# A shared ring for dwq and wq, four dK store buffers, and V^T of five batches by TensorE instead of by a transposing load

## The chip, the cores and the metric

One core of one Trainium2 chip. The metric is the device time of one execution in microseconds; a kernel's time is the median of several executions. Executions are compared with the kernel before on the same chip, in the same rounds. The chips differ: the kernel before takes 1650 us on some and 1642 on others, so ratios carry further here than times.

## The reference, cut to what matters

Two independent attention blocks A and B, whose outputs are concatenated, with all gradients. For each block, 8 batches of 96 queries, 32 heads of 128, 512 cached keys, model width 640, all bf16:

```python
q = (x @ wq).reshape(B, Sq, H, Dh).transpose(0, 2, 1, 3)
p = softmax(einsum("bhqd,bhkd->bhqk", q, k_cache) * Dh ** -0.5)
o = einsum("bhqk,bhkd->bhqd", p, v_cache)
out = o.transpose(0, 2, 1, 3).reshape(B, Sq, H * Dh) @ wo
# returned: out of both blocks, and the gradients of x, k_cache, v_cache, wq, wo of each
```

## The kernel before: the parts that the change touches

Heads go in pairs; a batch of a pair takes two ticks, some 6 us. Every transfer goes through one SyncE queue in program order. K and V come twice: natural, and transposed by the load. A transposing load of a pair, as this kernel makes it and reads it with correct results, leaves the keys in a peculiar order: 64 groups of 16, eight of one head and eight of the other.

```python
def p_ldT(h, b, which):          # KT or VT of two heads by a transposing load
    t_ = kvp.tile([128, F4 * KC, 16], BF16, name=key + "_p", bufs=5 if which == 0 else 4)
    sp(nc.sync.dma_start_transpose(t_[:], src))
    half = t_[:, :, j * R8:(j + 1) * R8]      # for each of the two heads: 8 of every 16
    CS[...][key] = half.rearrange("p (f c) r -> p f c r", c=KC)

def c_s6(h, b):                  # dP = dO V^T ; dS = (dP - dl) * P, reading dP in steps
    nc.tensor.matmul(dP_ps[:], hs["dOT_h"][:, tok], st["VT"], start=True, stop=True)
    nc.vector.scalar_tensor_tensor(dS_sb[:].rearrange("q (a f) -> q a f", f=F4),
        dP_ps[:].rearrange("q (f a) -> q a f", f=F4), dl_ps[:, 0:1], P_sb..., ...)

def c_s7(h, b):                  # dK of a pair, evacuated by ACT, stored by SyncE
    st["dK_p"] = wk.tile([128, HP, KC * 128], BF16, name="dK_sb", bufs=3)
def qD(h, c_lo, c_hi):           # dwq of a pair
    pr["dwq_sb"] = hd.tile([128, DC, HP * 128], BF16, name="dwq_sb", bufs=1)
# ... (the rest of the attention, projections and weight gradients left out)
```

## Time and profile before

| | before |
|---|---|
| median of 3 executions | 1650.46 us (1649.55 to 1652.88) |
| profiled execution, span | 1640.3 us |
| TensorE busy | 98% |
| granted clock, mean | 0.996 |

The lines that show the bound, the stretches and the stops stand in the prediction below. The columns are: line, engine, operation, output<-input, shapes, count | busy us, mean ns of one | idle us of the engine just before them, and what ended most of it.

```profile
L458 ACT ACTIVATE dK_sb<-dK_ps 128x512 bf16<-128x512 f32 x512 | 305.4, 597 | 149.6 <-PE dK_ps L453 130.9 <-DMA out_dram<-dK_sb 10.6 <-PE optp_ps L362 2.2
L362 PE MATMUL optp_ps<-PT_sb,V_sb 128*128 128x96 bf16 x2048 | 169.6, 204 | 3.0 <-ACT PT_sb L376 0.9 <-DMA V_sb<-in_A_v_cache_dram 0.8 <-DMA V_sb<-in_B_v_cache_dram 0.5
```

ACT waited 10.6 us in all for stores of dK, which is what the fourth buffer is for. TensorE waited almost nowhere for V loads: 3.0 us ahead of 512 products O^T.

### The profile page before, as it was taken

What the parts mean: (1) busy time and instruction counts of PE and PEld (TensorE: products, weight loads), DVE (VectorE), ACT (ScalarE), POOL (GpSimd) and SP (SyncE); (2) the same over time, 40 slices, a digit from 0 to 9 for tenths busy, and PEclk for the clock granted to TensorE, in tenths of its full rate; (3) what the DMA queues carried; (4) which work ended last, traced back from release to release, by engine and by line L of the source; (5) the groups of instructions that cost most, each with busy time, mean ns of one, the idle gap of its engine ahead of it and who ended that gap; (6) DMA issues with size and microseconds to landing.
All of it is one profiled execution on the core that took longest, in us unless ns stands there. A gap on an engine that the chain in (4) does not pass through costs nothing.

```text
span 1640.3 us, 55387 instructions
## 1 busy us (share of the span) xinstructions
PE 1602.0 (98%) x20713; PEld 1262.0 (77%) x20906; DVE 1340.0 (82%) x3406; ACT 1346.9 (82%) x3498; POOL 532.3 (32%) x1026
## 2 busy tenths in 40 slices
PE   8899999999999999999999999999999999999998
PEld 6777877878777787777777778777787777877776
DVE  5876888888888888878778778888888888888796
ACT  7889988879788788877868889788788888889783
POOL 1333333333333333333323333333333333333331
PEclk9999999999999999999999999999999999999999
DMA  9999999999999999999999999999999999999995
GB/s 263 261 293 273 292 291 282 275 275 279 276 292 289 290 280 282 280 276 258 284 289 311 289 288 273 290 290 283 275 287 278 272 290 287 281 292 285 284 267 167
DMA packets 375566, 458.12 MB, mean 279 GB/s; under 512 B 40704, under 2 KB 367104, under 8 KB 367104
## 3 DMA queue, kind: packets, MB, share of 16 engines
q1 hardware_dynamic: 375296, 454.57, 103.2%
q8 instruction: 163, 2.67, 0.7%
q14 instruction: 107, 0.88, 0.1%
HBM read 160.10 MB, written 159.12 MB: 195 GB/s over the span
## 4 chain that ended last, share of the span: by engine, by line
PE 89%; DMA 4%; ACT 4%; issue 2%; DVE 1%; SPq 0%; POOL 0%; ACTq 0%; DVEq 0%
PE o_ps L536 12%; PE q_ps L250 12%; PE dwq_ps L511 6%; PE dK_ps L453 6%; PE dV_ps L387 6%; PE S_ps L314 6%; PE dwo_ps L491 6%; PE dP_ps L411 6%; PE optp_ps L362 5%; PE optp_ps L369 5%; PE dq_dst_ps L430 5%; PE dq_dst_ps L437 5%; PE n_ps L265 3%; PE nat_ps L477 2%; DMA out_dram<-dK_sb 2%
## 5 line engine op out<-in xcount | busy, mean ns | idle before, releaser
L401 POOL TENSOR_TENSOR prod<-OT_h,dOT_h 128x96 bf16<-128x96 bf16 x512 | 187.1, 365 | 824.4 <-DVE rinv L336 438.2
L346 POOL TENSOR_SCALAR P_sb<-E_sb,rinv 96x512 bf16<-96x512 bf16 x508 | 349.8, 689 | 252.5 <-DVE rinv L336 252.1
L458 ACT ACTIVATE dK_sb<-dK_ps 128x512 bf16<-128x512 f32 x512 | 305.4, 597 | 149.6 <-PE dK_ps L453 130.9
L326 ACT ACTIVATE E_sb<-S_ps,negm 96x512 bf16<-96x512 f32 x512 | 350.9, 685 | 65.1 <-DVE negm L316 51.8
L316 DVE TENSOR_REDUCE negm<-S_ps 96x1 f32<-96x512 f32 x512 | 347.6, 679 | 67.2 <-PE S_ps L314 66.5
L415 DVE SCALAR_TENSOR_TENSOR dS_sb<-dP_ps,dl_ps,P_sb 96x512 bf16<-96x512 f32 x512 | 380.6, 743 | 1.6 <-PE optp_ps L369 1.4
L392 ACT ACTIVATE dV_sb<-dV_ps 128x512 bf16<-128x512 f32 x512 | 307.2, 600 | 3.9 <-PE dV_ps L387 2.6
L376 ACT ACTIVATE PT_sb<-optp_ps 128x384 bf16<-128x384 bf16 x512 | 255.2, 499 | 1.7 <-PE optp_ps L369 0.8
L439 DVE COPY dST_sb<-dq_dst_ps 128x384 bf16<-128x384 bf16 x512 | 177.5, 347 | 53.1 <-PE dq_dst_ps L437 51.5
L387 PE MATMUL dV_ps<-dOnat_h,P_sb 96*128 96x128 bf16 x2048 | 199.7, 219 | 2.1 <-DVE ob L546 1.0
L453 PE MATMUL dK_ps<-Qnat_h,dS_sb 96*128 96x128 bf16 x2048 | 198.9, 219 | 0.1
L411 PE MATMUL dP_ps<-VT_p,dOT_h 128*96 128x512 bf16 x512 | 195.8, 382 | 0.0
L314 PE MATMUL S_ps<-KT_p,QT_h 128*96 128x512 bf16 x512 | 194.0, 379 | 0.5 <-ACT E_sb L326 0.2
L453 PEld LDWEIGHTS <-dS_sb 96*128 96x128 bf16 x2048 | 147.5, 97 | 48.3 <-issue 0.6
L430 PE MATMUL dq_dst_ps<-dST_sb,K_sb 128*128 128x96 bf16 x2048 | 171.8, 205 | 3.0 <-ACT dK_sb L458 2.8
L369 PE MATMUL optp_ps<-ident,P_sb 96*128 96x96 bf16 x2048 | 172.4, 206 | 2.2 <-DVE P_sb L346 1.6
L362 PE MATMUL optp_ps<-PT_sb,V_sb 128*128 128x96 bf16 x2048 | 169.6, 204 | 3.0 <-ACT PT_sb L376 0.9
L437 PE MATMUL dq_dst_ps<-ident,dS_sb 96*128 96x96 bf16 x2048 | 171.8, 205 | 0.0
L536 PE MATMUL o_ps<-wo_r,OT_h 128*128 128x128 bf16 (+1 forms) x722 | 144.5, 294 | 2.4
L536 PE MATMUL o_ps<-wqT_h,dQT_h 128*128 128x512 bf16 (+1 forms) x720 | 144.2, 294 | 2.5
L362 PEld LDWEIGHTS <-V_sb 128*128 128x128 bf16 x2048 | 107.6, 96 | 50.7 <-issue 3.4
L491 PE MATMUL dwo_ps<-g_nat,Onat 128*128 128x128 bf16 (+1 forms) x735 | 129.4, 297 | 4.3 <-ACT dK_sb L458 2.6
(75 smaller groups left out, 3044.7 us busy)
## 6 DMA issues: line engine op xcount, KB each, us to landing
out_dram<-dV_sb SPq DMA_DIRECT2D x256, 256.0 KB, 4.4
out_dram<-dK_sb SPq DMA_DIRECT2D x256, 256.0 KB, 4.5
V_sb<-in_A_v_cache_dram SPq DMA_DIRECT2D x128, 256.0 KB, 4.3
K_sb<-in_A_k_cache_dram SPq DMA_DIRECT2D x128, 256.0 KB, 4.4
V_sb<-in_B_v_cache_dram SPq DMA_DIRECT2D x128, 256.0 KB, 4.3
K_sb<-in_B_k_cache_dram SPq DMA_DIRECT2D x128, 256.0 KB, 4.3
out_dram<-ob SPq DMA_DIRECT2D x88, 160.0 KB, 4.1
out_dram<-dwq_sb SPq DMA_DIRECT2D x32, 320.0 KB, 4.9
```

The source lines that it names most:

```text
L314: nc.tensor.matmul(S_ps[:], hs["QT_h"][:, tok], st["KT"], start=True, stop=True)
L316: nc.vector.tensor_reduce(negm[:], S_ps[:], axis=AX.X, op=ALU.max, negate=True)
L326: nc.scalar.activation(E_sb[:].rearrange("q (a f) -> q a f", f=F4), st["S_ps"][:].rearrange("q (f a) -> q a f", f=F4), ACT.Exp, bias=st["n ...
L346: eng.tensor_scalar(P_sb[:], st["E_sb"][:], st["rinv"][:], 0.0, op0=ALU.mult, op1=ALU.add)
L362: nc.tensor.matmul(OT_ps, st["V_sb"][:, c, :], st["PT_sb"][:, c * Sq:(c + 1) * Sq], start=(c == 0), stop=(c == KC - 1))
L387: nc.tensor.matmul(dV_ps[:, c * 128:(c + 1) * 128], P_sb[:, c * 128:(c + 1) * 128], hs["dOnat_h"][:, b * 128:(b + 1) * 128], start=True, s ...
L392: nc.scalar.activation(dV_p[:, j], dV_ps[:], ACT.Identity, scale=1.0)
L411: nc.tensor.matmul(dP_ps[:], hs["dOT_h"][:, tok], st["VT"], start=True, stop=True)
L415: nc.vector.scalar_tensor_tensor(dS_sb[:].rearrange("q (a f) -> q a f", f=F4), dP_ps[:].rearrange("q (f a) -> q a f", f=F4), dl_ps[:, 0:1] ...
L453: nc.tensor.matmul(dK_ps[:, c * 128:(c + 1) * 128], dS_sb[:, c * 128:(c + 1) * 128], hs["Qnat_h"][:, b * 128:(b + 1) * 128], start=True, s ...
L458: nc.scalar.activation(dK_p[:, j], dK_ps[:], ACT.Identity, scale=1.0)
L536: nc.tensor.matmul(o_ps[:], src[:, t * 128:(t + 1) * 128], rhs, start=(hh == 0), stop=(hh == groups[g] - 1))
```

## The change

The intent is to take load off the SyncE queue in the passage from block 1 to block 2, and to let its lag show less. dwq shares the ring of wq tiles, which pays for a fourth dK buffer. V^T of five batches of the last pair of block 1 is made by TensorE from the natural V, which is loaded anyway. dwo rows of the last three pairs of block 1 are stored one tick sooner.

```diff
+    def p_vT(h, b):
+            t_ = kvp.tile([128, F4 * KC, 16], BF16, name="VT_p", bufs=4)
+            v_ps = bank([128, HP * KC * 128], BF16, "vT_ps")
+            ... 8 x nc.tensor.transpose(v_ps[...128 columns...], V_sb[:, c, :], ident[:])
+            for j in range(HP):
+                half = t_[:, :, j * R8:(j + 1) * R8].rearrange("p (f c) r -> p f c r", c=KC)
+                evac("act" if j == 0 else "dve", half.rearrange("p f c r -> p c r f"),
+                     v_ps[:, j * KC * 128:(j + 1) * KC * 128].rearrange("p (c r f) -> p c r f", c=KC, f=F4))
-  name="dK_sb", bufs=3            ->  +  name="dK_sb", bufs=4
-  name="dwq_sb", bufs=1           ->  +  name="wq_p", bufs=2
-  em.add(ct + OFF["vt"], SLOTS["LOAD"], p_ldT(h, b, 1))
+  p_vT at ct + 4 where (blk, h, b) in pools["vpe"], else as before
-  qB_st(h) at max(hk["qB"]) + 2   ->  +  + 1 for the last three pairs of block 1
+  pools["vpe"] = {(0, NH - HP, b) for b in range(5)}
```

(Shortened; the arrows stand for one removed and one added line.) The evacuation walks its output in the order c, r, f, so that consecutive elements, 2 bytes each, are KC x 16 = 64 elements, that is 128 bytes, apart.

More of the change, by code (lines that the diff above doesn't have):

```diff
@@ L291, in p_ldn, with f @@
         return f
+    def p_vT(h, b):
+        def f():
+            t_ = kvp.tile([128, F4 * KC, 16], BF16, name="VT_p", bufs=4)
+            v_ps = bank([128, HP * KC * 128], BF16, "vT_ps")
+            for j in range(HP):
+                V_sb = CS[(blk, h + j, b)]["V_sb"]
+                for c in range(KC):
+                    nc.tensor.transpose(v_ps[:, (j * KC + c) * 128:(j * KC + c + 1) * 128], V_sb[:, c, :], ident[:])
+            for j in range(HP):
+                half = t_[:, :, j * R8:(j + 1) * R8].rearrange("p (f c) r -> p f c r", c=KC)
+                CS[(blk, h + j, b)]["VT"] = half
+                evac("act" if j == 0 else "dve", half.rearrange("p f c r -> p c r f"), v_ps[:, j * KC * 128:(j + 1) * KC * 128].rearrange("p (c r f) -> p c r f", c=KC, f=F4))
+        return f
     def p_st(h, b, which):
@@ L455, in f @@
             if j == 0:
-                st["dK_p"] = wk.tile([128, HP, KC * 128], BF16, name="dK_sb", bufs=3)
+                st["dK_p"] = wk.tile([128, HP, KC * 128], BF16, name="dK_sb", bufs=4)
             dK_p = CS[(blk, h - j, b)]["dK_p"]
@@ L504, in f @@
             if "dwq_sb" not in pr:
-                pr["dwq_sb"] = hd.tile([128, DC, HP * 128], BF16, name="dwq_sb", bufs=1)
+                pr["dwq_sb"] = hd.tile([128, DC, HP * 128], BF16, name="wq_p", bufs=2)
             n = c_hi - c_lo
@@ L580, in build_block @@
                     em.add(tick0 - 13 if early and b == 0 else ct + (max(OFF["kt"], -1) if early else OFF["kt"]), SLOTS["LOAD"], p_ldT(h, b, 0))
-                    em.add(ct + OFF["vt"], SLOTS["LOAD"], p_ldT(h, b, 1))
+                    if (blk, h, b) in pools["vpe"]:
+                        em.add(ct + 4, SL_HEAD, p_vT(h, b))
+                    else:
+                        em.add(ct + OFF["vt"], SLOTS["LOAD"], p_ldT(h, b, 1))
                     em.add(ct + OFF["vn"], SLOTS["LOAD"] + 0.1, p_ldn(h, b, 1))
@@ L601, in build_block @@
                 em.add(c0t + hk["qB"][min(di, len(hk["qB"]) - 1)], SL_HEAD + 1, qB(h, di))
-            em.add(c0t + max(hk["qB"]) + 2, SL_LOAD + 0.3, qB_st(h))
+            em.add(c0t + max(hk["qB"]) + (1 if first and h >= H - 3 * HP else 2), SL_LOAD + 0.3, qB_st(h))
             em.add(c0t + hk["qA1"], SL_HEAD, qA(h, 1))
```

## The prediction

> **What bounds the kernel now.** I read the engine shares of the page first, then the chain that ended last, then a table of 41 us stretches, then the TensorE instructions in order of time, and last the DMA issues of SyncE in the same stretches.
>
> The page:
>
> ```profile
> span 1640.3 us, 55387 instructions
> ...
> PE 1602.0 (98%) x20713; PEld 1262.0 (77%) x20906; DVE 1340.0 (82%) x3406; ACT 1346.9 (82%) x3498; POOL 532.3 (32%) x1026
> ...
> PE 89%; DMA 4%; ACT 4%; issue 2%; DVE 1%; SPq 0%; POOL 0%; ACTq 0%; DVEq 0%
> ```
>
> TensorE is the bound: 98% busy, 89% of the chain. Only 38.3 us of the span (1640.3 - 1602.0) is without it, so no removed wait can give more than that, 2.3%, plus what a lowered clock costs. Where the 38 us lie, by stretches (columns: length, busy time of PE, its weight loads, DVE, ACT, POOL with counts, granted clock, DMA share, GB/s):
>
> ```profile
> 41.00:82.00 41.00, 36.49 (x497) 29.70 (x497) 33.16 (x85) 36.20 (x99) 15.54 (x30) 0.96 1.07 261
> 697.00:738.00 41.00, 40.68 (x502) 31.36 (x506) 32.08 (x83) 32.80 (x85) 12.62 (x25) 1.00 1.06 277
> 738.00:779.00 41.00, 37.63 (x518) 30.40 (x520) 35.73 (x90) 29.62 (x77) 12.92 (x25) 1.00 1.06 258
> 779.00:820.00 41.00, 38.23 (x491) 30.73 (x497) 29.96 (x75) 35.15 (x92) 13.21 (x25) 0.96 1.03 283
> 861.00:902.00 41.00, 38.43 (x523) 30.29 (x526) 35.27 (x92) 35.03 (x92) 14.60 (x28) 1.00 1.07 307
> 902.00:943.00 41.00, 38.94 (x484) 30.21 (x485) 29.87 (x74) 33.51 (x89) 12.49 (x24) 0.96 1.06 293
> ```
>
> An ordinary stretch (697 to 738) loses 0.3 us. The loss is in the first 123 us, in the passage from block 1 to block 2 (738 to 943), and in the drain. The DMA share is above 1 in all, so the transfer stream runs close to its own limit. The stops of TensorE in the passage (start, length, what, idle before, releaser):
>
> ```profile
> 779.23 1.84 PE L159 MATMUL tp_ps<-ident,ob 128*128 128x128 bf16 x15 [2.90 <-ACT ob L170]
> 793.92 0.44 PE L220 MATMUL woT_ps<-ident,wo_r 128*128 128x128 bf16 x5 [1.79 <-ACT dK_sb L458]
> 844.41 0.38 PE L387 MATMUL dV_ps<-dOnat_h,P_sb 96*128 96x128 bf16 x4 [0.98 <-DVE ob L546]
> 896.50 0.34 PE L362 MATMUL optp_ps<-PT_sb,V_sb 128*128 128x96 bf16 x4 [0.48 <-DMA V_sb<-in_B_v_cache_dram]
> 918.41 0.38 PE L491 MATMUL dwo_ps<-g_nat,Onat 128*128 128x512 bf16 x1 [1.69 <-ACT dK_sb L458]
> ```
>
> TensorE waits for an evacuation, which itself waits for a buffer to be stored. ACT shows it:
>
> ```profile
> 778.90 0.28 ACT L170 ACTIVATE ob<-dwo_ps 128x128 bf16<-128x128 f32 x1 [3.67 <-DMA out_dram<-ob]
> 793.27 0.60 ACT L458 ACTIVATE dK_sb<-dK_ps 128x512 bf16<-128x512 f32 x1 [1.97 <-DMA out_dram<-dK_sb]
> ```
>
> Why were the stores late? All transfers go through one SyncE queue in program order, and there:
>
> ```profile
> 770.47 1.54 SPq L277 DMA_TRANSPOSE VT_p<-in_A_v_cache_dram  x1
> 772.10 0.53 SPq L288 DMA_DIRECT2D K_sb<-in_A_k_cache_dram  x1
> 772.72 0.42 SPq L297 DMA_DIRECT2D out_dram<-dK_sb  x1
> 773.20 0.46 SPq L497 DMA_DIRECT2D out_dram<-ob  x1
> 773.75 1.42 SPq L141 DMA_DIRECT2D ob<-in_grad_out_dram  x3
> ```
>
> No gaps: the queue issues back to back, 1.1 us or more for a transposing load against 0.4 to 0.5 for a plain one. The dK pair finished by ACT at 773.6 is stored only at 787.70, 14 us later, while in calm stretches this lag is 2 to 8 us. So the queue is behind, by the extra loads of block 2, and three store buffers no longer cover the lag.
>
> [...] a dK store takes a median 4.5 us from issue to landing, and its buffer is held that long. [...] after 2.90 us idle, 15 transposes take 1.84 us, against 1.00 at 759.66; the 8 us from 775 and the 8 us from 919 (after only 1.69 us idle) have a granted clock of 0.79, which is 1.7 us lost in each. [...] eight transposes (n_ps) occupy the chain for 0.45 us, 56 ns each. [...]
>
> **The change, part by part.** I compared the order of instructions on each engine. POOL is unchanged; TensorE gains only the transposes; ACT and DVE each gain five copies and a few neighbours change places; SyncE loses five transposing loads, and stores of dwo rows of the last three pairs of block 1 move ahead of about three transfers.
>
> 1. dwq in the wq ring. It frees 128x5x256 bf16, 2560 bytes a partition, and pays for the fourth dK buffer, 2048 bytes. By the emission ticks a wq tile's last reader is three ticks (about 9 us) before its buffer is asked for again, and dwq still follows the previous dwq's store by eleven ticks. I expect no wait: 0 us.
>
> 2. Four dK buffers. Each gives two more ticks, about 6 us, between a store and the reuse. Stops put down to dK: 1.79 at 794, then 0.24 + 0.72 + 0.54 + 1.69 = 3.2 between 882 and 918 with 1.7 us of low clock behind the last. In the first 110 us 0.32 + 2.81 + 0.28 + 0.90, of which I count 1.2: the long one (2.81 at 71.97) is followed at once by a V load that lands just when it is used, so there the wait only changes its name.
>
> 3. V^T by TensorE. Added: 5 batches x 8 transposes x 56 ns = 2.24 us on the bound engine, in full. Added on ACT 5 x about 0.6 us (as dK's 128x512 copy, 597 ns), on DVE 5 x about 0.5 us (128x640 copies take 480, the scattered store may cost more): 3 us each over 34 us, on engines about 82% busy. I allow 0.5 us of TensorE for it, since ACT is full from 783 to 791. Removed: the five loads at 752.66, 761.79, 770.47, 778.01, 784.86, with issue times 1.10, 1.17, 1.54, 2.26, 2.12, 8.2 us of the queue, and about 5 us of DMA time (estimate: 256 KB at the mean 279 GB/s, 0.94 us each). So the gradient loads and stores from 773 on come 3 to 4 us sooner, later ones 5 to 8.
>
> 4. The dwo store one tick sooner: 773.20 becomes about 769, so its buffer is free when ACT asks at 775.2. With the gradient loads also sooner, the stop of 2.90 us and 1.7 us of low clock should go, and the 0.98 us at 844 (also a store of this ring).
>
> Gross gain: 2.9 + 1.7 (776) + 1.8 (794) + 1.0 (844) + 3.2 + 1.7 (882 to 918) + 1.2 (start) = 13.5 us. Taken back: 2.24 for transposes, 0.5 for evacuations, about 1 because the fourth batch's transposes follow the gradient transposes at once and their V load (issued 776.36, landing 781.7) would come 1 us late even when issued 3.5 us sooner, and about 1.5 from 882 to 914, where V loads land 0.05 to 0.9 us before use, so without the dK stops TensorE reaches those loads sooner. Net 13.5 - 5.2 = 8.3 us; I round to 9, because the sooner queue should cover part of that last item. 1650.5 - 9 = 1641.5 us.
>
> **Rivals.**
> - *The feed is the true bound of the passage.* If SyncE and DMA run flat out from 738 to 943, then freed buffers only let TensorE reach late loads. For it: no gaps in the queue, DMA share above 1, slack of V loads 0.05 us at 896.5. Against: at 846 to 860 V loads land 5 to 11 us ahead, so the feed catches up there, and the removed loads relieve the same feed. Then only the 776 and 844 parts remain against 2.2 of cost: about 1647.
> - *The transposes cost more than they free.* They need V_sb about half a tick sooner than the first reader did, take a PSUM bank out of eight, and load ACT at its fullest. Each batch could stop TensorE for 0.5 to 1 us: 3 to 5 us back, time 1644 to 1650.
> - *The shared ring waits.* If a wq load waited for a dwq store, each pair could lose a few tenths, about 30 times: 1645 to 1655. The ticks speak against it.
> - *Everything clears,* with the start's 2.81 and its low clock too: about 1635.
>
> **Range and chances.** 1635 (all clears) to 1648.5 (feed-bound or dear transposes) should hold 8 of 10. Faster by over 2% means below 1617, more than nearly all idle time, 1%; slower by over 2% needs a wait repeated in all 32 pairs, 1%; within 2%, 98%.
>
> **What would show it.** Right if the stops at 776, 794 and 918 are gone, no ACT wait for a dK store is left in the passage, and the stretches 779 to 820 and 902 to 943 have clock 1.00; the vT_ps matmuls should sum to about 2.2 us of chain. Step 2 is wrong if as much idle stands there with V_sb or K_sb loads as releaser; step 3 if vT transposes wait for V_sb or their copies delay PT_sb; step 1 if a dwq copy or wq load shows waits for the other. An unchanged or longer time would mean the feed, not the buffers, sets the passage.

## The result, and the profile after

| | before | after |
|---|---|---|
| median, same rounds, 6 executions each | 1651.56 us | 1664.96 us (1658.18 to 1671.43) |
| ratio of fast runs, 95% interval | | 1.0078 (1.0050 to 1.0106) |

A ratio is the mean time of one kernel's fast runs over that of the other's fast runs of the same rounds, so it is not quite the ratio of the medians. The change is within 2%, as predicted, but slower, not faster, and outside the range. All executions compared here were fast; the mean granted clock of the profiled one was 0.994.

The page of the profiled execution after:

```profile
span 1663.1 us, 55473 instructions
...
PE 1607.5 (97%) x20752; PEld 1266.1 (76%) x20946; DVE 1352.5 (81%) x3411; ACT 1362.2 (82%) x3503; POOL 533.3 (32%) x1026
...
PE 86%; DMA 6%; ACT 3%; DVE 2%; issue 2%; POOL 0%; SPq 0%; DVEq 0%; ACTq 0%
```

Beside the page before, TensorE is busy 5.5 us more (slower clock included), and its share of the chain fell from 89% to 86%. The same stretches as in the prediction:

```profile
738.00:779.00 41.00, 37.53 (x463) 28.67 (x468) 31.32 (x77) 32.12 (x72) 11.54 (x22) 1.00 1.05 279
779.00:820.00 41.00, 31.35 (x347) 24.52 (x348) 30.01 (x57) 29.50 (x60) 8.36 (x16) 0.83 0.74 195
902.00:943.00 41.00, 38.84 (x535) 31.20 (x538) 33.72 (x86) 37.02 (x100) 15.02 (x29) 1.00 1.10 298
```

The stretch 779 to 820, which by the prediction should have gone to a clock of 1.00, fell to 0.83 and 31.35 us busy, and the DMA share fell from 1.03 to 0.74: the feed now waits too. The stretch 902 to 943 did get its full clock. The groups that answer to those of before, and the new copies:

```profile
L472 ACT ACTIVATE dK_sb<-dK_ps 128x512 bf16<-128x512 f32 x512 | 305.8, 597 | 136.1 <-PE dK_ps L467 133.2
L376 PE MATMUL optp_ps<-PT_sb,V_sb 128*128 128x96 bf16 x2048 | 169.9, 204 | 20.9 <-DMA V_sb<-in_A_v_cache_dram 9.7 <-DMA V_sb<-in_B_v_cache_dram 5.0 <-DVE VT_p L173 2.0
L170 ACT ACTIVATE VT_p<-vT_ps 128x512 bf16<-128x512 bf16 x5 | 12.3, 2462 | 0.0
L173 DVE COPY VT_p<-vT_ps 128x512 bf16<-128x512 bf16 x5 | 12.2, 2437 | 8.5 <-ACT VT_p L170 8.5
```

ACT's 10.6 us of waits for dK stores are no longer listed: that mechanism works. But each V^T copy takes 2.46 us on ACT and 2.44 on DVE where 0.6 and 0.5 were put, DVE waits for ACT's, and TensorE is idle 20.9 us ahead of O^T, mostly for V loads. So the trace shows two suspects: the copies, and a feed of loads that is late all over the run. Also in it: DMA packets of 16 KB (the transposing loads) took 1297 ns in the mean, 1255 in the trace before.

### The profile page after: what moved, and what is told of

Read it like the earlier page. It is cut to its first block, busy times and chain, and to the rows that moved or that the text cites.

```text
span 1663.1 us, 55473 instructions
## 1 busy us (share of the span) xinstructions
PE 1607.5 (97%) x20752; PEld 1266.1 (76%) x20946; DVE 1352.5 (81%) x3411; ACT 1362.2 (82%) x3503; POOL 533.3 (32%) x1026
## 4 chain that ended last, share of the span: by engine, by line
PE 86%; DMA 6%; ACT 3%; DVE 2%; issue 2%; POOL 0%; SPq 0%; DVEq 0%; ACTq 0%
PE o_ps L550 12%; PE q_ps L250 11%; PE dV_ps L401 6%; PE dwq_ps L525 6%; PE dK_ps L467 6%; PE S_ps L328 6%; PE dP_ps L425 6%; PE dwo_ps L505 6%; PE optp_ps L376 5%; PE optp_ps L383 5%; PE dq_dst_ps L444 5%; PE dq_dst_ps L451 4%; PE n_ps L265 3%; PE nat_ps L491 3%; DMA V_sb<-in_A_v_cache_dram 2%; DMA V_sb<-in_B_v_cache_dram 2%
## 5 line engine op out<-in xcount | busy, mean ns | idle before, releaser
L376 PE MATMUL optp_ps<-PT_sb,V_sb 128*128 128x96 bf16 x2048 | 169.9, 204 | 20.9 <-DMA V_sb<-in_A_v_cache_dram 9.7
L550 PE MATMUL o_ps<-wqT_h,dQT_h 128*128 128x128 bf16 (+1 forms) x719 | 144.7, 295 | 2.5
L387 DVE CAST OT_h<-optp_ps 128x96 bf16<-128x96 f32 x512 | 125.1, 244 | 14.2 <-PE optp_ps L383 13.8
```

The costliest lines, as they stand in the source:

```text
L376: nc.tensor.matmul(OT_ps, st["V_sb"][:, c, :], st["PT_sb"][:, c * Sq:(c + 1) * Sq], start=(c == 0), stop=(c == KC - 1))
L550: nc.tensor.matmul(o_ps[:], src[:, t * 128:(t + 1) * 128], rhs, start=(hh == 0), stop=(hh == groups[g] - 1))
```

## The experiments

Sixteen runs were made, all with correct results. The table has fifteen of them; the before time is that of the same rounds.

| label | what | median us | before us | ratio, 95% interval |
|---|---|---|---|---|
| ring_only | shared ring alone | 1641.16 | 1641.24 | 0.9994 (0.9978 to 1.0010) |
| qb_only | sooner dwo store alone | 1640.16 | 1643.38 | 0.9989 (0.9975 to 1.0004) |
| no_vt | all but V^T by TensorE | 1639.12 | 1641.24 | 0.9985 (0.9973 to 0.9998) |
| vt_only | V^T by TensorE alone | 1655.44 | 1641.24 | 1.0079 (1.0059 to 1.0100) |
| after_again | the whole change | 1653.22 | 1641.89 | 1.0062 (1.0041 to 1.0083) |
| vt_dense | whole change, dense V^T | 1633.82 | 1641.24 | 0.9949 (0.9930 to 0.9968) |
| vt_swap | whole change, copy loops turned | 1633.17 | 1641.89 | 0.9943 (0.9924 to 0.9963) |
| vt_dense_only | dense V^T alone | 1635.53 | 1641.89 | 0.9965 (0.9949 to 0.9981) |
| vt_long | dense, copies repeated | 1644.41 | 1643.38 | 1.0011 (0.9995 to 1.0028) |
| vt_chunk | scattered, in four pieces | 1658.62 | 1650.30 | 1.0058 (1.0038 to 1.0078) |
| vt_later | scattered, DVE's copy later | 1648.73 | 1642.38 | 1.0043 (1.0028 to 1.0057) |
| vt_act | scattered, both on ACT | 1654.76 | 1642.38 | 1.0082 (1.0059 to 1.0105) |
| more_start | vt_swap, 9 batches | 1631.63 | 1643.38 | 0.9925 (0.9896 to 0.9954) |
| more_both | vt_swap, 13 batches | 1628.31 | 1643.38 | 0.9909 (0.9881 to 0.9937) |
| dense_both | vt_dense, 13 batches | 1635.39 | 1650.30 | 0.9909 (0.9894 to 0.9923) |

(before_again, a single execution for its trace, state unknown, took 1649.79 us.) The expectations of no_vt, vt_only, vt_dense and ring_only, in us, were written against the 1650 us of the first executions; on the chip of these runs the kernel before takes 1641, so ratios are to be compared. A first theory, A, says that the copies are the whole loss; B, that a slower feed from the ring or the fourth buffer is half of it; C, that the slower feed belongs to the execution and not to the program.

### Which part costs

**no_vt** and **vt_only** split the change in two.

```diff
  no_vt:    pools["vpe"] = set()                       # on the kernel after
  vt_only:  before + p_vT and pools["vpe"] of the kernel after; dK_sb bufs=3, dwq_sb bufs=1
```

> The changed kernel without the five V^T by TensorE (shared ring, four dK buffers and the earlier dwo store stay). Theory A (the two scattered copies of 2.45 us per batch, one after the other on ACT and DVE, are the whole loss, and what they shift also causes the waits for V loads elsewhere): 1641 to 1647 us, the stretch 779 to 820 has TensorE busy 38 us or more, and idle ahead of the OT matmuls on V loads falls back from 20.9 to about 3 us. Theory B (the loss has two halves: the copies near 780, and a slower feed in the whole run that comes from the shared ring or the fourth dK buffer): 1651 to 1657 us, idle on V loads stays near 15 to 20 us, and the 16 KB packets of the transposing loads stay near 1297 ns against 1255 before. Theory C (the slower feed is only a matter of the execution, not of the program): packets and V waits differ between the executions of one kernel, and the time spreads by 0.5% or more.

> The kernel before with only the five V^T by TensorE (own dwq buffer, three dK buffers, dwo store at its old place). Theory A: 1659 to 1664 us, nearly the whole loss. Theory B: 1655 to 1659 us, that is the copies alone (about 4.9 us for each batch in series, of which some 1 to 1.5 us reach TensorE), V waits near 3 us and 16 KB packets near 1255 ns. The two stops on dK stores at 794 and 918 of the kernel before should come back.

Measured 0.9985 and 1.0079: V^T by TensorE is the whole loss, and the rest of the change a small gain. In us, no_vt came below A's range and vt_only into B's, 1655 to 1659; as a ratio, vt_only fits A (1659 to 1664 beside 1650 is 1.0055 to 1.0085), and no_vt lies by 0.0003 above A (0.9945 to 0.9982) and well below B (1.0006 to 1.0042). Its trace was taken in one of its fastest executions (its 22 executions lie between 1631.75 and 1643.62), so only the names of its waits are used here:

```profile
887.79 0.34 PE L376 MATMUL optp_ps<-PT_sb,V_sb 128*128 128x96 bf16 x4 [0.96 <-DMA V_sb<-in_B_v_cache_dram]
...
908.77 0.42 PE L425 MATMUL dP_ps<-VT_p,dOT_h 128*96 128x512 bf16 x1 [2.08 <-DMA VT_p<-in_B_v_cache_dram]
```

(Columns: start, length, engine, line, operation and tiles, count, idle before it and releaser.) Where the kernel before stopped for dK stores, this one stops for loads. That is what was said in the first rival of the prediction: freed buffers let TensorE reach late loads. For comparison the kernel before, traced again on the chip of the later experiments:

> The kernel before, for a trace from the same chip as the experiments: 1637 to 1646 us. Shows whether its stops on dK and dwo stores (776, 794, 918) are there in every execution, or come and go with the feed: theory C expects other stops of similar sum, since its times on this chip spread from 1635 to 1649 us.

```profile
894.53 0.38 PE L387 MATMUL dV_ps<-dOnat_h,P_sb 96*128 96x128 bf16 x4 [1.97 <-ACT dK_sb L458]
907.57 0.61 PE L265 MATMUL n_ps<-ident,dOT_h 128*96 128x128 bf16 x8 [0.88 <-ACT dK_sb L458]
926.10 0.38 PE L491 MATMUL dwo_ps<-g_nat,Onat 128*128 128x512 bf16 x1 [2.01 <-ACT dK_sb L458]
```

Its stops on dK are there again, somewhat longer; the one execution was slower than expected by 4 us, and with an unknown state only the names of its waits are used.

**ring_only** and **qb_only** split no_vt further.

```diff
  ring_only (on before):  - name="dwq_sb", bufs=1    + name="wq_p", bufs=2
  qb_only (on before):    - qB_st at max(hk["qB"]) + 2    + + 1 for the last three pairs of block 1
```

> The kernel before with only dwq moved to the ring of wq (three dK buffers). Theory A: 1649 to 1652 us, no change. Theory B with the ring as cause of the slow feed: 1656 to 1661 us with V waits of 10 us or more. Theory B with the fourth dK buffer as the cause: 1649 to 1652 us, V waits near 3 us.

> The kernel before with only the earlier store of the dwo rows of the last three pairs of block 1. The prediction gave this and the sooner queue 5.6 us; the change without V^T (ring, four dK buffers and this store) gained only 0.15%, 2.5 us. If the store is its own gain: 0.997 to 0.9985, and the stop near 780 on ob is gone. If without the removed loads the ob buffer is still late, or the wait only changes its name: 0.9985 to 1.001.

The ring is free: 0.9994. The sooner store alone is 0.9989, not to be told from none; in its trace TensorE still stands 2.27 us ahead of the gradient transposes at 778, with the gradient load itself as releaser. That load was behind this stop from the first. In the trace before, PE's record names ACT's evacuation, but the weight loads of the same transposes (PEld) had waited 3.07 us for the load:

```profile
779.23 1.57 PEld L159 LDWEIGHTS <-ob 128*128 128x128 bf16 x15 [3.07 <-DMA ob<-in_grad_out_dram]
```

And before_again, without the sooner store, stops there for 2.67 us with the load as releaser. With no_vt at 0.9985, the fourth dK buffer, which was not run alone, adds nothing that these intervals show.

### The slow feed

**after_again** is the changed kernel on another chip.

> The changed kernel once more, on a chip where the kernel before takes about 1641 us. Its first trace had two losses: stops near 780 and waits for V loads all over, with 16 KB packets at 1297 ns. If the second belongs to the execution (theory C), this trace has the 16 KB packets at 1230 to 1260 ns and the idle ahead of the OT matmuls at 6 to 12 us instead of 20.9, and the time against before is still 1.005 to 1.010, since the copies alone gave 1.0079. If the second belongs to the program (shared ring, four dK buffers and copies together), the packets stay near 1297 ns and the idle near 20 us.

The ratio repeats, 1.0062, but the idle ahead of O^T is half of that in the first trace, and the loads no longer lead the list:

```profile
L376 PE MATMUL optp_ps<-PT_sb,V_sb 128*128 128x96 bf16 x2048 | 169.6, 204 | 10.7 <-DVE VT_p L173 2.6 <-ACT PT_sb L390 2.5 <-DMA V_sb<-in_B_v_cache_dram 2.4
```

The 16 KB packets are at 1238 ns, against 1297 in the first trace and 1230 to 1278 in those of the other runs that I compared. So C holds for the waits for V all over the first trace: they are not in every execution of this program. Whether the chip or the execution makes them is not shown. The ratio does not hang on them, since it comes out alike with (1.0078) and without (1.0062); but they made the first pair of traces misleading: the profiled execution before took 1642.09 us, while those timed beside the kernel after took 1650 to 1653. What made that feed slower is open.

### What in V^T costs

**vt_dense** keeps V^T in the order in which the transposes leave it, so both copies run straight through. **vt_swap** keeps the old order of V^T and turns the loops of the copy: it writes runs of eight elements and reads PSUM in steps.

```diff
  vt_dense:  half = flat[:, j * KC * 128:(j + 1) * KC * 128]
             evac("act" if j == 0 else "dve", half, v_ps[:, j * KC * 128:(j + 1) * KC * 128])
             # and dP of these batches is read in natural order
  vt_swap:   - evac(..., half.rearrange("p f c r -> p c r f"), v_ps[...].rearrange("p (c r f) -> p c r f", ...))
             + evac(..., half, v_ps[...].rearrange("p (c r f) -> p f c r", ...))
```

> The changed kernel with the same five batches by TensorE, but V^T kept in the order in which the transposes leave it, so that both copies write consecutive elements, and dP of these batches is read in natural order. Both theories: each copy falls from 2.45 us to 0.5 to 0.7 us, and TensorE's stops at 770, 782, 794, 804 and 815 on VT_p, rinv and PT_sb shrink to less than 2 us in all. Theory A: 1641 to 1648 us. Theory B: the V waits of the rest stay, 1651 to 1657 us. If the copies stay above 2 us, the scattered write is not what makes them slow.

> The changed kernel with the loops of the two V^T copies turned round: they read PSUM in steps and write eight consecutive elements (16 bytes) at a time, into the same interleaved V^T. If the scattered writing is what makes a copy 2.45 us: copies of 0.5 to 0.8 us and about 1634 to 1640 us, as with the dense V^T. If any order other than consecutive on both sides is dear: copies of 2 us or more and 1650 to 1656 us. In both cases DVE still waits for ACT[...]; if that series alone were the loss, the time would stay above 1648 us even with short copies.

The copies of vt_dense, then of vt_swap:

```profile
L170 ACT ACTIVATE VT_p<-vT_ps 128x512 bf16<-128x512 bf16 x5 | 3.1, 614 | 0.0
...
L173 DVE COPY VT_p<-vT_ps 128x512 bf16<-128x512 bf16 x5 | 2.1, 418 | 1.2 <-ACT VT_p L170 1.0
```

```profile
L173 DVE COPY VT_p<-vT_ps 128x512 bf16<-128x512 bf16 x5 | 3.4, 685 | 1.2 <-ACT VT_p L170 1.0
...
L170 ACT ACTIVATE VT_p<-vT_ps 128x512 bf16<-128x512 bf16 x5 | 3.0, 610 | 0.0
```

This settles what makes the copies long: the scattered writing. The same 512 elements for each of 128 partitions, into the same interleaved tile, take 0.61 us on ACT instead of 2.46 when eight consecutive elements are written at a time; DVE takes 0.69 instead of 2.44. Beside the dense copy, runs of eight with a PSUM read in steps cost ACT nothing (610 ns of one against 614) and DVE 0.27 us (685 against 418). And both kernels are faster than before, 0.9949 and 0.9943. The stretches of vt_swap, to be laid beside those of the kernel after:

```profile
738.00:779.00 41.00, 40.51 (x567) 33.11 (x566) 37.76 (x95) 32.99 (x86) 13.18 (x26) 1.00 1.05 279
779.00:820.00 41.00, 40.55 (x536) 32.26 (x534) 33.78 (x84) 35.33 (x93) 13.26 (x26) 1.00 1.06 284
```

Both are nearly full and at full clock: the long stops, the low clock and the stalled feed are all gone. (Runs of other lengths than one and eight elements were not tried.)

**vt_dense_only** is the same dense V^T on the kernel before, without the other parts.

> The kernel before with only the five V^T by TensorE, stored densely (three dK buffers, own dwq buffer, dwo store at its old place). The dense form of the whole change gave 0.9949, the change without V^T 0.9985. If the parts add up: 0.9964, that is 1633 to 1638 us beside 1641. If V^T by TensorE only pays once the buffers are free: 0.998 or more.

It measured 0.9965, just where the parts add up. So the removed loads, not the buffers, bring most of the gain: 0.35% alone, 0.51% with the rest. With its three dK buffers this kernel's trace has 2.4 us of TensorE stops behind dK left between 738 and 943; the trace before has 5.0.

### How long copies stop TensorE

The chain can be read in after_again, at the first of the five batches:

```profile
752.13 0.61 PE L300 MATMUL vT_ps<-ident,V_sb 128*128 128x128 bf16 x8
...
753.01 0.15 DVE L350 RECIPROCAL rinv<-rowsum 96x1 f32<-96x1 f32 x1
...
753.54 2.47 ACT L170 ACTIVATE VT_p<-vT_ps 128x512 bf16<-128x512 bf16 x1
...
756.05 2.43 DVE L173 COPY VT_p<-vT_ps 128x512 bf16<-128x512 bf16 x1 [2.89 <-ACT VT_p L170]
...
758.10 0.62 DVE L330 TENSOR_REDUCE negm<-S_ps 96x1 f32<-96x512 f32 x1
...
758.53 0.33 PE L376 MATMUL optp_ps<-PT_sb,V_sb 128*128 128x96 bf16 x4 [2.63 <-DVE VT_p L173]
...
758.82 0.68 ACT L340 ACTIVATE E_sb<-S_ps,negm 96x512 bf16<-96x512 f32 x1 [2.39 <-DVE negm L330]
...
771.74 0.16 PE L427 MATMUL dl_ps<-ones,prod 128*96 128x1 bf16 x1 [1.45 <-DVE VT_p L173]
```

DVE stands at its copy from 753.2, waits 2.9 us for ACT's, and copies until 758.5. The row maximum (negm) of scores that TensorE had begun at 754.09 stands behind the copy and starts only at 758.10, and ACT's exp waits for that. The stop of 2.63 us, though, does not go through negm: its releaser is the copy itself. In the passage the trace has six stops of over 1 us, of two kinds. Three wait for the end of the copy: 2.63, 1.45 and 1.29 (ahead of nat_ps at 783.30), 5.4 us in sum; these matmuls do not read V^T, and each starts 0.05 us after DVE's copy has ended. Three wait for what stood behind a copy on its engine, PT_sb on ACT or rinv on DVE: 1.67, 2.88 and 1.49, 6.0 us in sum. Together 11.4 us, with granted clocks of 0.92 and 0.88 in the stretches 738 to 779 and 779 to 820. Low clock is worth at most 41 x (0.08 + 0.12) = 8.2 us (an estimate, the mean includes idle time), so at most 19.6 us in all, against (1.0062 - 0.9943) x 1641.9 = 19.5 us between after_again and vt_swap. That the two agree so closely is chance, since single traces differ by some us at the start alone. A count inside the passage does without the start: from the 237th to the 257th of the 512 row maxima (negm), all of which every trace has, it is 83.5 us in after_again and 63.0 in vt_swap, a difference of 20.5.

Four runs ask which property of the two copies does it. **vt_long**: short dense copies, repeated until they last as long. **vt_chunk**: scattered copies in four pieces. **vt_later**: DVE's copy placed behind the next row maximum. **vt_act**: both copies on ACT.

```diff
  vt_long  (on vt_dense):  + for _ in range(4 if j == 0 else 6):  evac(...)
  vt_chunk (on after):     + for c in range(KC):  evac(..., half[:, :, c].rearrange("p f r -> p r f"), v_ps[... chunk c ...])
  vt_later (on after):     + DVE's copy emitted at ct + 5, ordered after negm of batch b + 1
  vt_act   (on after):     - evac("act" if j == 0 else "dve", ...)    + evac("act", ...)
```

> The changed kernel with the dense V^T, whose copies are made long on purpose: ACT makes its copy four times (4 x 0.61 = 2.45 us), DVE its copy six times (6 x 0.42 = 2.5 us), all with consecutive elements. If the length of the two copies, one after the other, is what costs the time, whatever makes them long: 1650 to 1656 us, ratio 1.004 to 1.009, with the stops near 780 to 815 on VT_p, PT_sb and rinv and the low clock back. If the scattered writing disturbs something else (other readers or writers of the memory), the time stays below 1645 us although both engines are as busy as in the changed kernel.

> The changed kernel, scattered as it is, but each of the two copies of a batch cut into four (a chunk of 128 columns each, about 0.6 us), with the same elements written to the same places. Busy time of ACT and DVE is that of the changed kernel, about 2.5 us each per batch. If half of the loss is that a copy of 2.45 us can't be interrupted (exp, PT_sb and rinv of the same moment wait behind it): 1.000 to 1.003 as with the long dense copies (1.0011), with other instructions between the pieces. If the scattering, or DVE's wait for ACT, costs by itself: 1.005 to 1.009 as the changed kernel.

> The changed kernel, scattered, but DVE's copy of each batch emitted one tick later and held behind the row maximum of the next batch, so that DVE does not stand with its copy at the head while ACT is still at its own. In the build this moves the copies of the first two batches behind two to seven other instructions, those of the last three by few or none. If half of the loss is DVE's idle wait for ACT (10.1 us in the run with pieces): the idle falls to 5 us or less and the ratio to 1.001 to 1.004. If the undivided lengths or the scattering are what counts: 1.005 to 1.008 again.

> The changed kernel, scattered, with both copies of a batch on ACT, one after the other (4.9 us of ACT, none of DVE, so no wait between engines). If DVE's wait for ACT is the other half of the loss: 1.001 to 1.004. If it is the 4.9 us in series that TensorE sees, whichever engine does them: 1.005 to 1.010.

- vt_long fell between its two theories: 1.0011. The same busy time on both engines (12.0 and 12.3 us, mean 600 and 412 ns of one) costs (1.0011 - 0.9949), about 10 us beside vt_dense, half of what the scattered copies cost. In its trace other instructions stand between the repeated copies. By the count inside the passage it takes 71.5 us, vt_dense 62.9.
- vt_chunk, 1.0058, did not test what it was built for: the build left the pieces of a copy mostly next to each other, and DVE still stood idle for ACT's last one:

```profile
L173 DVE COPY VT_p<-vT_ps 128x128 bf16<-128x128 bf16 x20 | 12.5, 868 | 10.1 <-ACT VT_p L170 10.1
```

- vt_act, 1.0082, takes away the wait between the engines and keeps 4.9 us in series. The loss stays (80.8 us by the count), so that wait is not its cause by itself. The stops ahead of the same matmuls are there again, now until ACT's second copy has ended:

```profile
779.24 0.16 PE L427 MATMUL dl_ps<-ones,prod 128*96 128x1 bf16 x1 [1.35 <-ACT VT_p L170]
```

- vt_later cuts DVE's idle time ahead of its copies from 8.6 to 3.4 us and gives 1.0043, between its two theories; its interval still overlaps that of after_again (78.6 us by the count).

What these leave: the length of the copies costs in both forms (about 10 us with consecutive writes in vt_long, 18 to 20 with scattered ones), and more where they hold an engine without a break; vt_long's gaps and vt_later's order both point that way. How the second half divides between unbroken length and order is not settled. Nor is why the O^T product at 758.53 waits for the copy itself. The program has eight PSUM banks in rotation (its pool ps, bufs=8) and vT_ps keeps one until both copies are done, so a bank may be what it waits for; vt_act, where such stops end with the last copy on the other engine, fits that. But in vt_long vT_ps is in use from 755.5 to 765.4, and the O^T product of the next tick starts at 759.17 without a wait. No trace tells which bank a tile has, so this was only argued.

### A version that beats both

The trace of vt_swap still stops TensorE for late loads at the start. Columns of the stretch as before:

```profile
60.00:80.00 20.00, 15.13 (x195) 12.54 (x193) 13.33 (x34) 14.55 (x39) 6.20 (x12) 0.83 1.06 291
```

So V^T was made by TensorE there too.

```diff
  more_start (on vt_swap):   + | {(0, 0, b) for b in (5, 6, 7)} | {(0, HP, 0)}
  more_both  (on more_start):+ | {(1, HP, b) for b in range(2, 6)}
  dense_both:                the thirteen batches of more_both on vt_dense
```

> The kernel with the turned copy loops (0.9943), and V^T by TensorE also for four batches at the start (batches 5 to 7 of the first pair and batch 0 of the second), where its trace has TensorE stop for V^T, K and V loads at 63 to 74, 4.9 us idle and a clock of 0.83 in the stretch 60 to 80. If the late queue is what stops TensorE there: about 4 us less idle and 3 us less of low clock, against 1.8 us of transposes: 0.990 to 0.993. If ACT, busy 19.6 of 20 us in the stretch ahead of it, can't take the copies: 0.994 to 0.997.

> As the one with four batches more at the start, and batches 2 to 5 of the second pair of block 2 as well, ahead of the V loads that stopped TensorE by 1.0 and 1.2 us at 907 and 926. 2.2 us idle to win against 1.8 us of transposes: within 0.001 of the run without them. If the TensorE time is the true price everywhere, slightly slower.

> The dense V^T with the thirteen batches of the fastest run so far (0.9909 with turned loops, whose DVE copy takes 0.69 us against 0.42 dense). If DVE's 0.27 us per batch matter: 0.988 to 0.990. If DVE has room there: 0.990 to 0.992, the same.

The same stretch in more_both:

```profile
60.00:80.00 20.00, 17.86 (x271) 14.89 (x271) 18.34 (x49) 19.22 (x54) 8.47 (x17) 1.00 1.10 287
```

In this trace the low clock is gone and 2.7 us more of the stretch are busy. One trace proves little there: after_again, which makes no V^T by TensorE at the start, has 18.80 us busy and a clock of 1.00 in the same stretch. More_start is at 0.9925, more_both and dense_both at 0.9909, the fastest; of DVE's 0.27 us per copy nothing is seen. The intervals of more_start and more_both both overlap that of vt_swap, and each other's. What shows a gain of the eight batches more is dense_both: its interval, 0.9894 to 0.9923, lies below that of vt_dense, 0.9930 to 0.9968. How it divides between the start and block 2 is not shown.

## Why the prediction was wrong

The step that failed is a term of step 3, "Added on ACT 5 x about 0.6 us (as dK's 128x512 copy, 597 ns), on DVE 5 x about 0.5 us (128x640 copies take 480, the scattered store may cost more)", with "I allow 0.5 us of TensorE for it". Both sizes in it were off. The durations were taken from copies of the same size that write consecutively; the runs show 2.46 and 2.44 us, in series, four to five times as much. And the price to TensorE, 0.5 us, rested on engines that the working called about 82% busy, as if they had room; the runs show 18 to 20 us: 1.0079 - 0.9965 of 1641 us is 18.7 on the kernel before, 19.5 on the kernel after, and even consecutive copies of that length cost about 10 (vt_long). With short copies the change gives 0.9949, which is 8.4 us of 1641, beside a predicted net gain of 8.3 us. That the two agree is partly luck: the buffers and the sooner store brought less than the sum has for them, the removed loads more.

- *Bound:* right. TensorE stayed the bound, and what the change gained or lost in the passage was idle time and clock of it.
- *Step 1, ring, 0 us:* right, 0.9994 (0.9978 to 1.0010).
- *Step 2, fourth dK buffer, some 8 us:* the waits for dK stores went, as predicted, but the gain did not come from there. no_vt gains 0.15%, 2.5 us, for the buffer, the ring and the sooner store in sum. Rival 1 had it right: behind the freed buffers stand late loads.
- *Step 3, removed loads:* under-valued. They were put down as relief for the queue that lets the other steps pay; by themselves they are 5.7 us net of their cost (0.9965), with the buffers and the store as before. The trace of that run has no low clock after 776, but neither has that of ring_only, so this sign alone shows little. The transposes cost TensorE what was put: in vt_swap the next matmul starts 0.45 us after each batch's first one, 2.2 us in five.
- *Step 4, sooner store, 2.9 + 1.7 and 0.98 us:* wrong by itself. Alone it is 0.9989 (0.9975 to 1.0004), and the stop at 778 remains, waiting for the gradient load. The working read the stop of 2.90 us from PE's record alone and missed the 3.07 us for that load in the record of the weight loads.
- *Rival 2, dear transposes:* right in kind ("Each batch could stop TensorE for 0.5 to 1 us"), too small in size: the stops are 1.3 to 2.9 us each, and the clock falls behind them (0.92 and 0.88 in the two stretches of after_again). One of the prediction's own signs, that "their copies delay PT_sb", is there at 781.15 in after_again (1.67 us).
- *Range:* its top of 1648.5 allowed the feed or "dear transposes" some 7 us. A single written doubt, "the scattered store may cost more", carried no number, so the range never opened for it.

What would have caught it: a run of the copy in both orders before its price was put, as vt_dense and vt_swap were run later. The copy wrote one bf16 per 128 bytes. In these runs eight bf16 at a time take the time of the dense copy on ACT (0.61 us), and one at a time does not (2.46): 4.8 ns for each of 512 columns on ACT and on DVE (2462 / 512 and 2437 / 512), against 1.2 and 1.3 in runs of eight (610 / 512 and 685 / 512). Even half of the measured durations, 1.2 us, would have put the copies far beyond 0.5 us. The kernel before had a hint as well: the DVE step of c_s6 (743 ns of one) reads the keys' peculiar order in steps and writes it consecutively.

## What to carry to other kernels

Before moving a layout change from a transfer to an engine's copy, look at the innermost step of what the copy writes, and try the steps on the side that reads PSUM: here that took the copies from 2.4 to 0.7 us or less. Price a copy by a copy with the same pattern, not by one of the same size (2.46 us against 597 ns on ACT here); a long unbroken copy delays what stands behind it on its engine, even where the engine has idle time on average (DVE was 81% busy in the trace after, and in after_again a row maximum whose scores began at 754.09 started at 758.10, behind a copy of 2.43 us). Read a stop of TensorE in the records of its weight loads too, before naming its cause (here 3.07 us for the gradient load behind 2.90 us put down to ACT). And in this kernel, whose queue was late, taking work out of the queue gained more (0.35%) than buffers and a sooner store that let the lag show less (0.15%).
